# Two fully connected layers after a decaying attention: the second layer's products cut into halves of the array's rows

## The chip, the cores and the metric

One core of a Trainium2 chip (trn2) runs the whole program. The metric is device microseconds of one execution. Three runs of the kernel before took 862.36, 862.7 and 864.8 us (median 862.7). A TensorE product multiplies a stationary 128-row weight tile with moving columns; its sum goes to a bank of PSUM. The array can also be addressed as tiles of 64 of its 128 rows, which then hold weights of their own.

## The reference

Four sequences of 768 tokens and 8 heads of 48 pass a linear attention with decay; its 384 features per token pass two fully connected layers of width 2048, each `h = x @ w_in`, a pointwise function, `g @ w_out`:

```
h = x @ w_in;  g = max(h, 0) + alpha * min(h, 0);        x = g @ w_out     # first layer
h = x @ w_in;  g = h * tanh(log(1 + exp(h)));            out = g @ w_out   # second layer
```

## The kernel before

Each float32 operand is split into two float32r parts, high and low, and each product is made three times (`PASSES`: high by high, high by low, low by high). All sums are kept in float32.

The 3072 tokens are handled as 6 chunks of 512 columns, and the width as 16 blocks of 128: a layer has 96 slots, one for a chunk and a block. In a slot the **inner product** (tile `h`, one PSUM bank, two buffers) takes 3 row blocks x 3 passes = 9 products of 128 x 512 (`emit_h`, L269). The pointwise function makes g and its two parts `ghiB`, `gloB`. The **output sum** takes 3 banks (`acc0` to `acc2`, or `sc` and `yt` in turn) x 3 passes = 9 products of 128 x 512 (L690 in layer one, L817 in layer two). In the last chunk of layer two the operands change places, and a slot has 4 banks x 3 passes = 12 products of 128 x 384 (L815).

The work of the first layer and of the attention stands in an order by a table of places. Layer two, which the change touches, is written by the loop at the end: it goes in pairs of slots. For slots n and n + 1 it emits both inner products, then for each of the two the pointwise instructions (`mish`) and the output sum of four slots earlier (`LAG_B = 4`; in the first four slots these are the last four output sums of layer one). Each engine runs its instructions in the order in which they are emitted.

`mish(n)` has six ACT instructions (tanh of slot n, the first; a square of slot n; the high part of g of slot n - 2; two squares of slot n - 1 and one of slot n) and five of DVE (g of n - 2, b of n - 1, a of n, which is the last reader of bank `h`, the low part of g of n - 2, c of n - 1). The profile names these by the buffers that they share: tanh is `m`, its square `ghi`, the other squares `glo` and `s`. `split_x2` adds an ACT and a DVE instruction in three of 16 slots. `mB_turn` (DVE transposes, L825) empties a chunk's three banks after its last output sum; the last chunk's fourth bank is one of the two `sc` banks that the chunk before it has filled. `mB_last` orders the last two output sums bank by bank. GpSimd has two late weight splits (`w2_split`, emitted at slots 6 and 8) and no other work in layer two.

## Time and profile before

| | |
|---|---|
| median of 3 runs | 862.7 us |
| the profiled execution, its own time | 864.74 us |
| its span, first to last instruction | 862.8 us |
| TensorE busy | 854.3 us (99%) |
| DVE, ACT, GpSimd busy | 629.9, 612.3, 115.1 us |
| granted TensorE clock | 1.0 |

A timeline row holds the instructions of one kind that follow each other without a pause: start, length, count. A product's row is as long as it takes until its last column has left the array, so rows of products overlap, and the distance of their starts is what a product costs. An instruction's idle time before it, and what ended that, stand in brackets.

### The profile page before, as it was taken

What the parts mean: (1) busy time and instruction counts of PE and PEld (TensorE: products, weight loads), DVE (VectorE), ACT (ScalarE), POOL (GpSimd) and SP (SyncE); (2) the same over time, 40 slices, a digit from 0 to 9 for tenths busy, and PEclk for the clock granted to TensorE, in tenths of its full rate; (3) what the DMA queues carried; (4) which work ended last, traced back from release to release, by engine and by line L of the source; (5) the groups of instructions that cost most, each with busy time, mean ns of one, the idle gap of its engine ahead of it and who ended that gap; (6) DMA issues with size and microseconds to landing.
All of it is one profiled execution on the core that took longest, in us unless ns stands there. A gap on an engine that the chain in (4) does not pass through costs nothing.

```text
span 862.8 us, 16681 instructions
## 1 busy us (share of the span) xinstructions
PE 854.3 (99%) x6382; PEld 709.8 (82%) x6382; DVE 629.9 (73%) x969; ACT 612.3 (71%) x1170; POOL 115.1 (13%) x133
## 2 busy tenths in 40 slices
PE   9999999999999999999999999999999999999998
PEld 6887888888888888888888888888888888888897
DVE  8889776666656656444666887887887887887875
ACT  5987555445545445543556989989989998998886
POOL 5465641112211112100002000000000000000000
PEclk9999999999999999999999999999999999999999
DMA  9886734364255434223520300110110110100101
GB/s 347 260 247 179 223 99 133 96 206 135 84 163 162 147 85 171 66 65 120 172 78 15 111 1 1 32 43 1 30 45 1 29 47 0 30 9 1 28 10 38
DMA packets 65328, 79.95 MB, mean 93 GB/s; under 512 B 39648, under 2 KB 52448, under 8 KB 65248
## 3 DMA queue, kind: packets, MB, share of 16 engines
q1 hardware_dynamic: 64688, 78.78, 30.4%
q8 instruction: 50, 0.82, 0.4%
q14 instruction: 30, 0.25, 0.1%
q10 hardware_dynamic: 560, 0.10, 0.1%
HBM read 61.16 MB, written 15.73 MB: 89 GB/s over the span
## 4 chain that ended last, share of the span: by engine, by line
PE 92%; DVE 2%; ACT 2%; DMA 2%; issue 1%; POOL 0%; SPq 0%; DVEq 0%; ACTq 0%; POOLq 0%
PE h L269 43%; PE acc L690 21%; PE sc L817 8%; PE acc L817 8%; PE yt L817 4%; PE acc L815 2%; PE sc L501 1%; DMA nat<-in_nat 1%; PE h L532 1%; PE sc L815 1%; PE yt L553 1%; PE sc L546 1%; DMA cst<-in_consts 1%; PE yt L532 1%; ACT wrawr L216 0%
## 5 line engine op out<-in xcount | busy, mean ns | idle before, releaser
L269 PE MATMUL h<-x,w 128*128 128x512 f32 (+1 forms) x1746 | 415.5, 387 | 2.1 <-DVE x L190 1.9
L269 PEld LDWEIGHTS h<-x,w 128*128 128x128 f32 x1746 | 325.0, 188 | 69.7 <-issue 2.5
L690 PE MATMUL acc<-ghi,w 128*128 128x512 f32 x516 | 174.9, 394 | 0.0
L658 ACT ACTIVATE m<-h 128x512 f32<-128x512 f32 x96 | 57.1, 595 | 92.8 <-PE h L269 92.7
L660 DVE SCALAR_TENSOR_TENSOR g<-m,oma,h 128x512 f32<-128x512 f32 x96 | 71.6, 746 | 60.2 <-ACT m L658 59.2
L690 PEld LDWEIGHTS acc<-ghi,w 128*128 128x128 f32 x516 | 96.8, 188 | 21.3
L187 ACT ACTIVATE ghi<-g 128x512 fp32r<-128x512 f32 x86 | 54.2, 630 | 74.9 <-PE acc L690 48.0
L690 PE MATMUL acc<-glo,w 128*128 128x512 f32 x258 | 100.4, 389 | 0.0
L190 DVE TENSOR_TENSOR glo<-g,ghi 128x512 fp32r<-128x512 f32 x86 | 62.8, 730 | 51.5 <-ACT ghi L187 51.2
L754 DVE SCALAR_TENSOR_TENSOR a<-ghi,h 128x512 f32<-128x512 f32 x96 | 66.0, 687 | 38.5 <-ACT ghi L751 32.0
L754 DVE SCALAR_TENSOR_TENSOR g<-s,c 128x512 f32<-128x512 f32 x95 | 66.6, 701 | 22.5 <-ACT s L751 20.4
L762 ACT ACTIVATE m<-h 128x512 f32<-128x512 f32 x96 | 56.4, 588 | 35.6 <-PE h L269 35.6
L190 DVE TENSOR_TENSOR gloB<-g,ghiB 128x512 fp32r<-128x512 f32 x105 | 72.0, 685 | 7.1 <-ACT ghiB L187 7.1
L751 ACT ACTIVATE ghi<-m,biases 128x512 f32<-128x512 f32 x96 | 69.6, 725 | 3.2
L187 ACT ACTIVATE ghiB<-g 128x512 fp32r<-128x512 f32 x105 | 64.8, 617 | 9.1 <-PE acc L690 6.9
L751 ACT ACTIVATE glo<-ghi,biases 128x512 f32<-128x512 f32 x96 | 68.1, 709 | 0.1
L751 ACT ACTIVATE s<-glo,biases 128x512 f32<-128x512 f32 x96 | 68.1, 709 | 0.0
L751 ACT ACTIVATE s<-s,biases 128x512 f32<-128x512 f32 x96 | 68.0, 708 | 0.0
L817 PE MATMUL sc<-ghiB,w 128*128 128x512 f32 x192 | 66.9, 389 | 0.0
L754 DVE SCALAR_TENSOR_TENSOR b<-ghi,a 128x512 f32<-128x512 f32 x96 | 65.6, 684 | 0.1
L754 DVE SCALAR_TENSOR_TENSOR c<-glo,b 128x512 f32<-128x512 f32 x95 | 65.7, 691 | 0.0
L817 PE MATMUL acc<-ghiB,w 128*128 128x512 f32 x192 | 61.7, 389 | 0.0
(189 smaller groups left out, 1148.3 us busy)
## 6 DMA issues: line engine op xcount, KB each, us to landing
wrawr<-in_w SPq DMA_DIRECT2D x28, 768.0 KB, 5.3
nat<-in_nat SPq DMA_DIRECT2D x40, 288.0 KB, 4.4
w2d<-wj SPq DMA_DIRECT2D x16, 384.0 KB, 2.5
wraw<-w2d SPq DMA_DIRECT2D x16, 384.0 KB, 3.1
rk<-in_rkT SPq DMA_DIRECT2D x40, 128.0 KB, 3.1
x2d<-xo SPq DMA_DIRECT2D x6, 768.0 KB, 3.2
x<-x2d SPq DMA_DIRECT2D x6, 768.0 KB, 4.6
rk<-in_rkT SPq DMA_DIRECT2D x40, 96.0 KB, 2.8
```

What stands on the lines that cost most here:

```text
L187: act.activation(out=hi, in_=src, func=AF.Copy)
L190: eng.tensor_tensor(out=lo, in0=src, in1=hi.bitcast(F32), op=ALU.subtract)
L269: pe.matmul(h[:, n], w_in(layer, f, a, c), x[:, b, c, n], start=(k == 0), stop=(k == 3 * KC - 1))
L532: pe.matmul(y[i][64 * q:64 * q + 64, p * HC:(p + 1) * HC], T[ROWS[h], 2 * bp + i, k, :], pair[i][ROWS[h], 0, k, t], start=(r == 0 and not ...
L658: act.activation(out=m, in_=hA[s], func=AF.Relu, scale=-1.0)
L660: dve.scalar_tensor_tensor(out=g, in0=m, scalar=oma[:, f:f + 1], in1=hA.pop(s), op0=ALU.mult, op1=ALU.add)
L690: pe.matmul(acc[0][c], w_out(0, f, a)[:, c * 128:(c + 1) * 128], g[b], start=(f == 0 and k == 0), stop=(f == NF - 1 and k == 2))
L751: act.activation(out=out, in_=in_, func=AF.Square, scale=scale, bias=fin[bias])
L754: dve.scalar_tensor_tensor(out=out, in0=in0, scalar=scalar, in1=in1, op0=op0, op1=ALU.mult)
L762: act.activation(out=bnew("t", n), in_=v["h", n], func=AF.Tanh, scale=0.5)
L815: pe.matmul(acc[1][t][:, :DM], g[a][:, t * C:(t + 1) * C], w_out(1, f, b), **se)
L817: pe.matmul(acc[1][t], w_out(1, f, a)[:, t * 128:(t + 1) * 128], g[b], **se)
```

## The change

Layer two's main loop goes slot by slot, and each of its products is cut along the rows that it sums over: one product of rows 0 to 63 and one of rows 64 to 127, each with its own weight load. `rows_slot` writes two lanes, top and low. Top has the upper half of the slot's inner product, then the upper half of the output sum; low has first three lower halves left from the slot before, then the lower half of the output sum, then the lower half of the inner product but for its last three. The lanes are merged by a count of columns. So the two halves of one bank are never written at the same time: the first half's last product releases an event on GpSimd (`pool.nop()`, ordered behind it), and the second half's first product waits for that event. A slot has five such events, in the last chunk six (one for each bank of the output sum, one for the inner product, and one ahead of the next slot's output sum). `follow(m)`, with the pointwise work of slot m, comes once the three left products are issued. The last four output sums, two before `mB_last` and two in it, stay whole products.

TensorE, slot 4 of layer two. Before: the inner products of slots 4 and 5 (weights `w_5213`, `w_5236`), then the output sum of slot 0 (`w_5080`).

```order
L269 MATMUL h<-x,w_5213 128x512 [waits DVE_49]
L269 MATMUL h<-x,w_5213 128x512 x8
L269 MATMUL h<-x,w_5236 128x512 [waits DVE_49]
L269 MATMUL h<-x,w_5236 128x512 x8
L817 MATMUL sc<-ghiB,w_5080 128x512 [waits Activation_49]
L817 MATMUL sc<-gloB,w_5080 128x512
L817 MATMUL sc<-ghiB,w_5080 128x512 x2
L817 MATMUL sc<-gloB,w_5080 128x512
L817 MATMUL sc<-ghiB,w_5080 128x512
L817 MATMUL yt<-ghiB,w_5080 128x512
```

The same slot now. Halves of one product read alike; in a pair one is of the upper rows and one of the lower.

```order
L293 MATMUL sc<-ghiB,w_5080 128x512 [waits Pool_sequencer_49,Activation_49]
L293 MATMUL h<-x,w_5213 128x512
L293 MATMUL sc<-gloB,w_5080 128x512 [waits DVE_49]
...
L293 MATMUL sc<-gloB,w_5080 128x512
L293 MATMUL h<-x,w_5213 128x512
L293 MATMUL sc<-ghiB,w_5080 128x512
L293 MATMUL sc<-ghiB,w_5080 128x512 [waits Pool_sequencer_49]
L293 MATMUL yt<-ghiB,w_5080 128x512
L293 MATMUL sc<-gloB,w_5080 128x512
L293 MATMUL yt<-gloB,w_5080 128x512
L293 MATMUL sc<-ghiB,w_5080 128x512
L293 MATMUL yt<-ghiB,w_5080 128x512
L293 MATMUL sc<-ghiB,w_5080 128x512 [waits Pool_sequencer_49]
```

The output sum of slot 0 now lies beside the inner product of slot 4, and its second halves wait for GpSimd's event (`Pool_sequencer`).

DVE, where chunk 4's banks are emptied. Before:

```order
L754 SCALAR_TENSOR_TENSOR c<-glo,b 128x512
L825 STREAM_TRANSPOSE ot<-sc 128x512 [waits DMAHW4_49,DMAHW5_49,DMAHW3_49,DMAHW6_49,DMAHW2_49,DMAHW7_49,DMAHW0_49,PE_49]
L754 SCALAR_TENSOR_TENSOR g<-s_9139,c 128x512 [waits DVE_49,Activation_49]
L754 SCALAR_TENSOR_TENSOR b<-ghi,a 128x512
L754 SCALAR_TENSOR_TENSOR a<-ghi,h 128x512 [waits DVE_49,Activation_49]
L190 TENSOR_TENSOR gloB<-g,ghiB 128x512 [waits Activation_49]
L754 SCALAR_TENSOR_TENSOR c<-glo,b 128x512
L825 STREAM_TRANSPOSE ot<-sc 128x512
```

Now:

```order
L821 SCALAR_TENSOR_TENSOR c<-glo,b 128x512
L894 STREAM_TRANSPOSE ot<-sc 128x512 [waits PE_49]
L894 STREAM_TRANSPOSE ot<-sc 128x512
L821 SCALAR_TENSOR_TENSOR g<-s_11088,c 128x512 [waits DVE_49,Activation_49]
L821 SCALAR_TENSOR_TENSOR b<-ghi,a 128x512
L821 SCALAR_TENSOR_TENSOR a<-ghi,h 128x512 [waits DVE_49,Activation_49]
L190 TENSOR_TENSOR gloB<-g,ghiB 128x512 [waits Activation_49]
L821 SCALAR_TENSOR_TENSOR c<-glo,b 128x512
```

Both transposes of `sc` stand in one slot's work, where they stood in two.

TensorE, from the last inner product to `mB_last`. Before (`h` is slot 95's, then the output sums of slots 90, 91, 92, 93):

```order
L269 MATMUL h<-x,w_5163 128x512 x8
L815 MATMUL acc_9211<-w_5428,ghiB 128x384 [waits Activation_49]
...
L815 MATMUL acc_9211<-w_5730,ghiB 128x384 [waits Activation_49]
...
L815 MATMUL acc_9211<-w_5817,ghiB 128x384 [waits Activation_49]
...
L815 MATMUL acc_9211<-w_5043,ghiB 128x384 [waits Activation_49]
```

Now (the end of slot 95, its three left products, then the output sums of slots 92, 93 and, with `w_5062`, 94):

```order
L293 MATMUL h<-x,w_5163 128x512
L293 MATMUL sc<-w_5894,gloB 128x384
L293 MATMUL h<-x,w_5163 128x512 x3
L749 MATMUL acc_11059<-w_6027,ghiB 128x384 [waits Activation_49]
...
L749 MATMUL acc_11059<-w_5043,ghiB 128x384 [waits Activation_49]
...
L749 MATMUL acc_11059<-w_5062,ghiB 128x384 [waits Activation_49]
```

Two output sums stand behind the last inner product ahead of `mB_last`, where there were four.

```diff
--- before.py
+++ after.py
@@ -260,6 +260,67 @@
 
     PASSES = ((0, 0), (0, 1), (1, 0))
 
+    def h_products(layer, f, x, h):
+        steps = [(c, a, b) for c in range(KC) for a, b in PASSES]
+        return [(h, w_in(layer, f, a, c), x[:, b, c], k == 0, k == 3 * KC - 1) for k, (c, a, b) in enumerate(steps)]
+
+    def order(behind, ahead):
+        tc.add_manual_dep(behind.ins, ahead.ins.name,
+                          mybir.DependencyInfo(mybir.DependencyClass.Sync, mybir.DependencyReason.DATA), reason="turns")
+
+    late = 3
+    lower = {"h": [], "o": None}
+
+    def rows_slot(h, o):
+
+        nh, no = len(h), len(o)
+        per_bank = len(PASSES)
+        top = [("h", k, 0) for k in range(nh)] + [("o", k, 0) for k in range(no)]
+        low = [("o", k, 1) for k in range(no)] + [("h", k, 1) for k in range(nh)]
+        keep = low[len(low) - late:] if nh else []
+        low = [("tail", k, 1) for k in range(len(lower["h"]))] + low[:len(low) - len(keep)]
+        tail, lower["h"] = lower["h"], [h[k] for _, k, _ in keep]
+        marks = {}
+        mark_low = 6 if no > 3 * per_bank else 5
+        base = nh - len(keep)
+        clock = [0, 0]
+        lanes = [top, low]
+        while top or low:
+            lane = 0 if top and (not low or clock[0] <= clock[1]) else 1
+            kind, k, half = lanes[lane].pop(0)
+            out, w, x, start, stop = (tail if kind == "tail" else h if kind == "h" else o)[k]
+            first = lane if kind == "o" else 1 - lane
+            mm = pe.matmul(out, w[HALF[half]], x[HALF[half]], start=start and (lane == (kind == "o")),
+                           stop=stop and (lane != (kind == "o")))
+            clock[lane] += x.shape[-1]
+            mark = wait = None
+            if kind == "h" and lane == 0 and k == nh - 1:
+                mark = "h"
+            elif kind == "o" and lane == 1 and k % per_bank == per_bank - 1:
+                mark = "o", k // per_bank
+            elif lane == 1 and ((kind == "h" and k == mark_low) or (kind == "tail" and base_of[0] + k == mark_of[0])):
+                mark = "low"
+            if kind == "h" and lane == 1 and k == 0:
+                wait = marks["h"]
+            elif kind == "o" and lane == 0 and k % per_bank == 0:
+                wait = marks["o", k // per_bank]
+            elif kind == "o" and lane == 1 and k == 0:
+                wait = lower["o"]
+            if mark:
+                marks[mark] = pool.nop()
+                order(marks[mark], mm)
+                if mark == "low":
+                    lower["o"] = marks[mark]
+            if wait:
+                order(mm, wait)
+            if kind == "tail" and k == len(tail) - 1:
+                yield
+        base_of[0], mark_of[0] = base, mark_low
+        if not tail:
+            yield
+
+    base_of, mark_of = [0], [0]
+
     def emit_h(layer, f, x, h, n=slice(0, 512), which=None):
         steps = [(c, a, b) for c in range(KC) for a, b in PASSES]
         if which is not None:
@@ -681,14 +742,19 @@
         gA[s] = (hi, lo)
 
     def mA_out(s):
+        whole(out_products(s))
+
+    def whole(products):
+        for o, w, x, start, stop in products:
+            pe.matmul(o, w, x, start=start, stop=stop)
+
+    def out_products(s):
         blk, f = A_SLOTS[s]
         if f == 0:
             acc[0] = [bank(f"acc{c}") for c in range(KC)]
         g = gA.pop(s)
-        for c in range(KC):
-            for k, (a, b) in enumerate(PASSES):
-                pe.matmul(acc[0][c], w_out(0, f, a)[:, c * 128:(c + 1) * 128], g[b],
-                          start=(f == 0 and k == 0), stop=(f == NF - 1 and k == 2))
+        return [(acc[0][c], w_out(0, f, a)[:, c * 128:(c + 1) * 128], g[b], f == 0 and k == 0, f == NF - 1 and k == 2)
+                for c in range(KC) for k, (a, b) in enumerate(PASSES)]
 
     def mA_end(blk):
         o = per.tile([128, KC, 512], F32, tag="wraw", name="xo", bufs=NRAW)
@@ -736,7 +802,8 @@
 
     def mB_h(s):
         j, f = B_SLOTS[s]
-        v["h", s] = emit_h(1, f, fin["x", j], bank("h", 2))
+        v["h", s] = bank("h", 2)
+        return h_products(1, f, fin["x", j], v["h", s])
 
     OLD = {"t": "m", "gb": "g", "q": "ghi", "s1": "glo"}
 
@@ -808,13 +875,15 @@
         if f == 0:
             acc[1] = acc_B[j] = banks_B(j)
         g = v["g", s]
+        products = []
         for t in parts if j == NCH - 1 else range(KC):
             for k, (a, b) in enumerate(PASSES):
-                se = dict(start=(f == 0 and k == 0), stop=(f == NF - 1 and k == 2))
+                se = f == 0 and k == 0, f == NF - 1 and k == 2
                 if j == NCH - 1:
-                    pe.matmul(acc[1][t][:, :DM], g[a][:, t * C:(t + 1) * C], w_out(1, f, b), **se)
+                    products.append((acc[1][t][:, :DM], g[a][:, t * C:(t + 1) * C], w_out(1, f, b)) + se)
                 else:
-                    pe.matmul(acc[1][t], w_out(1, f, a)[:, t * 128:(t + 1) * 128], g[b], **se)
+                    products.append((acc[1][t], w_out(1, f, a)[:, t * 128:(t + 1) * 128], g[b]) + se)
+        return products
 
     def mB_turn(j, c):
 
@@ -848,7 +917,7 @@
     def mB_last():
 
         for s, t in ((2, 0), (2, 1), (1, 0), (2, 2), (1, 1), (2, 3), (1, 2), (1, 3)):
-            mB_out(NB - s, (t,))
+            whole(mB_out(NB - s, (t,)))
             if s == 1:
                 mB_end(NCH - 1, (t,))
 
@@ -1022,37 +1091,39 @@
         run_plan()
 
 
-        for n in range(0, NB + LAG_B, 2):
-            pair = range(n, n + 2)
-            for m in pair:
-                if m < NB:
-                    mB_h(m)
-            if n == 0:
-                mA_hi(NA - 1)
-                mA_lo(NA - 1)
-            for m in pair:
-                if m < LAG_B:
-                    mA_out(NA - LAG_B + m)
-                mish(m)
-                if m == LAG_B - 1:
-                    mA_end(NCH - 1)
-                if m in (6, 8):
-                    w2_split(11 + (m - 6) // 2, pool)
-                if m == 4:
-                    load_x2(1)
-                if m == NB + LAG_B - 1:
-                    mB_last()
-                elif LAG_B <= m < NB + LAG_B - 2:
-                    mB_out(m - LAG_B)
-                    j, f = divmod(m - LAG_B + 1, NF)
-                    if j and f < KC:
-                        mB_turn(j - 1, f)
-                if m < NB:
-                    j, f = B_SLOTS[m]
-                    if f in (5, 7, 9) and j + 1 < NCH:
-                        split_x2(j + 1, (f - 5) // 2)
-                    if f == 10 and j + 2 < NCH:
-                        load_x2(j + 2)
+        def follow(m):
+
+            mish(m)
+            if m == LAG_B - 1:
+                mA_end(NCH - 1)
+            if m in (6, 8):
+                w2_split(11 + (m - 6) // 2, pool)
+            if m == 4:
+                load_x2(1)
+            j, f = divmod(m - LAG_B + 1, NF)
+            if j and f < KC and m < NB + LAG_B - 2:
+                for c in (range(2), (), (2,))[f] if j == NCH - 1 else (f,):
+                    mB_turn(j - 1, c)
+            if m < NB:
+                j, f = B_SLOTS[m]
+                if f in (5, 7, 9) and j + 1 < NCH:
+                    split_x2(j + 1, (f - 5) // 2)
+                if f == 10 and j + 2 < NCH:
+                    load_x2(j + 2)
+
+        mA_hi(NA - 1)
+        mA_lo(NA - 1)
+        for m in range(NB):
+            for _ in rows_slot(mB_h(m), mB_out(m - LAG_B) if m >= LAG_B else out_products(NA - LAG_B + m)):
+                if m:
+                    follow(m - 1)
+        for _ in rows_slot([], []):
+            follow(NB - 1)
+        for m in range(NB, NB + LAG_B):
+            if m < NB + LAG_B - 2:
+                whole(mB_out(m - LAG_B))
+            follow(m)
+        mB_last()
 
 
 # ---- launch: one core ----
```

## Rows read from the trace of the kernel before

**Rows 1.** The page's first lines: the span, and each engine's busy time.

```profile
span 862.8 us, 16681 instructions
...
PE 854.3 (99%) x6382; PEld 709.8 (82%) x6382; DVE 629.9 (73%) x969; ACT 612.3 (71%) x1170; POOL 115.1 (13%) x133
```

**Rows 2.** Chain that ended last: start us, us, engine, tile, line, count.

```profile
600.14 4.08 PE acc L817 x18
```

**Rows 3.** By shape, PE: line, operation, shape, count | busy us, mean ns | idle.

```profile
L269 PE MATMUL h<-x,w 128*128 128x512 f32 x1710 | 410.6, 390 | 2.1 <-DVE x L190 1.9 <-DVE w L190 0.2
...
L269 PE MATMUL h<-x,w 128*128 128x256 f32 x36 | 4.8, 288 | 0.0
...
L377 PE MATMUL acc<-RK,cst 64*48 64x256 f32 x2 | 0.6, 376 | 0.0
```

**Rows 4.** Timeline, PE, the opening: start us, us, engine, line, operation, shape, count.

```profile
27.73 2.68 PE L269 MATMUL h<-x,w 128*128 128x256 f32 x21
```

**Rows 5.** By shape, PE, 5.8 to 7 us, the warm-up products in float32.

```profile
L641 PE MATMUL acc<-ghi 128*128 128x384 f32 x5 | 1.8, 486 | 0.0
```

**Rows 6.** Timeline, PE, the same warm-up products.

```profile
5.29 2.10 PE L641 MATMUL acc<-ghi 128*128 128x384 f32 x6
```

**Rows 7.** Timeline, PE: float32 products in tiles of 64 rows, 64 columns.

```profile
10.38 0.61 PE L377 MATMUL acc<-RK,cst 64*48 64x256 f32 x8
...
117.75 0.65 PE L501 MATMUL sc<-rk 48*64 48x64 f32 x32
118.22 0.49 PE L546 MATMUL sc<-nat 64*48 64x48 f32 x27
```

**Rows 8.** Timeline, 380.17 to 380.75 us: TensorE, GpSimd, TensorE.

```profile
380.17 0.22 PE L532 MATMUL yt<-rk,T 48*64 48x64 f32 x1
380.54 0.11 POOL L536 MEMSET T<- 112x8 f32 x1 [17.47 <-PE yt L532]
380.70 0.13 PEld L532 LDWEIGHTS yt<-rk,T 48*64 48x64 f32 x1 [0.46 <-POOL T L536]
```

**Rows 9.** Timeline, ACT, the end of one slot and the start of the next.

```profile
603.00 0.62 ACT L187 ACTIVATE ghiB<-g 128x512 fp32r<-128x512 f32 x1
...
606.30 0.60 ACT L762 ACTIVATE m<-h 128x512 f32<-128x512 f32 x1 [0.84 <-PE h L269]
...
607.56 0.61 ACT L187 ACTIVATE ghiB<-g 128x512 fp32r<-128x512 f32 x1
```

**Rows 10.** Timeline, DVE, beside them.

```profile
607.69 0.69 DVE L754 SCALAR_TENSOR_TENSOR a<-ghi,h 128x512 f32<-128x512 f32 x1 [0.71 <-ACT ghi L751]
608.29 0.69 DVE L190 TENSOR_TENSOR gloB<-g,ghiB 128x512 fp32r<-128x512 f32 x1
```

**Rows 11.** Timeline, PE, the change from whole products to tiles.

```profile
115.79 1.75 PE L269 MATMUL h<-x,w 128*128 128x512 f32 x7
117.47 0.27 PE L532 MATMUL h<-rk,T 48*64 48x64 f32 x1
```

**Rows 12.** Timeline, GpSimd, the two last weight splits.

```profile
457.41 0.82 POOL L236 CAST w<-wraw 128x768 fp32r<-128x768 f32 x1 [68.61 <-PE acc L690]
458.32 2.17 POOL L190 TENSOR_TENSOR w<-wraw,w 128x768 fp32r<-128x768 f32 x1
```

**Rows 13.** Timeline, DVE, the last chunk's first slots.

```profile
805.34 0.71 DVE L825 STREAM_TRANSPOSE ot<-sc 128x512 f32<-128x512 f32 x1
```

**Rows 14.** Timeline, PE, the same place.

```profile
806.10 0.62 PE L815 MATMUL sc<-w,ghiB 128*128 128x384 f32 x2 [0.37 <-DVE ot L825]
```

**Rows 15.** Timeline, ACT, the end.

```profile
847.94 0.57 ACT L762 ACTIVATE m<-h 128x512 f32<-128x512 f32 x1
...
853.86 0.63 ACT L187 ACTIVATE ghiB<-g 128x512 fp32r<-128x512 f32 x1 [0.70 <-DVE g L754]
```

**Rows 16.** Timeline, DVE, the end.

```profile
854.52 0.69 DVE L190 TENSOR_TENSOR gloB<-g,ghiB 128x512 fp32r<-128x512 f32 x1 [0.44 <-ACT ghiB L187]
```

**Rows 17.** Timeline, PE, the end.

```profile
855.27 0.44 PE L815 MATMUL acc<-w,gloB 128*128 128x384 f32 x1
```

## The prediction

> **What bounds the kernel now.** I read the page's first lines, then the chain of waits, then products by shape, then timelines of single places. TensorE is busy 854.3 of 862.8 us [rows 1], at a granted clock of 1.0 throughout, the 2.4 GHz level, so the time is the number of products by the distance of their starts. In layer two 18 products of 512 columns take 4.08 us [rows 2], 226.7 ns each. A column per cycle makes 213.3 ns; 13.4 are left. They don't depend on the width: 21 products of 256 columns lie in 2.68 us, the last alone being 288 ns long [rows 3, 4], so 119.6 ns from start to start, of which 106.7 are columns and 12.9 are not. Float32 products of the whole array, with a weight load each, hardly have this part: six of 384 columns in 2.10 us, the last 486 ns [rows 5, 6], are 323 ns apart, 320 of them two cycles a column. So some 13 ns per product belong to float32r on the whole array, and the reader should see that only they can be won: nothing in TensorE's row is a wait.
>
> The next engine is ACT. From the high part at 603.00 to its idle time (0.84 us before 606.30) are 2.46 us, and from tanh at 606.30 to the next high part 1.26 [rows 9]: 3.7 us a slot against 4.08. It has room down to that.
>
> **What the change does, part by part.** *Products.* Halves are made of 96 x 9 inner products, 4 x 9 output sums of layer one, 80 x 9 of 512 columns and 12 x 12 of 384 in layer two: 1764. Two halves side by side need as many cycles as one whole product, if the tiles run at once. No float32r tile of 64 rows is in the trace, so I bound its step from both sides. That tiles run at once is shown in float32: 32 products of 64 columns in four tiles take 118.22 - 117.75 = 0.47 us, 59 ns for four, where columns alone would be 4 x 53 in sequence [rows 7]. What they lose at a change of weights is small: eight of 256 columns lie in 0.61 us, the last 376 ns long [rows 3, 7], so the second round of four starts about 0.22 us after the first, 213.3 for columns and 3 to 7 ns more; by the 59 ns it is 5. One end is therefore 216 ns for a pair (3 lost), the other 227 to 229 (the 13 ns stay in each tile, some ns for twice the instructions). The nearest row by form, two row tiles in turn, is the 3 to 7 ns: I take 218, a saving of 8.7 ns by 1764 products = **15.3 us** (216: 18.9; 220: 11.8; 228: -2.3). A slot is then 18 x 0.218 = 3.92 us, still above ACT's 3.7.
>
> The Trainium skill (TensorE: Matmul & The Clock Gate, Back-to-back issue gap) gives 2.5 ns beyond the columns as the gap between products, so 215.8 for 512. The 226.7 above do not follow it, the float32 rows do; by that rule in both tiles the saving would be 19.2 us, about my fast end.
>
> *Events.* Each event lies four pairs ahead of its waiter, 0.87 us. The way through GpSimd is in the attention: a product that starts at 380.17 and ends at 380.39, the memset at 380.54 for 0.11, the next load at 380.70 [rows 8]: 0.15 to GpSimd and 0.05 back, with 0 to 0.11 for the event itself. With the product's own 0.39 [rows 3] that is 0.59 to 0.70 us. Its weight load takes under 0.12 (256-column products come every 119.6 ns with one load each), so it may start 0.75 after the event's product. I take no wait. If the load has to stand a full pair ahead (0.65), up to 0.05 us is lost at the four places of a slot where TensorE waits for events: 0.05 x 4 x 96 = 19 us is the other end. Behind a waiting product the whole TensorE queue stands, both lanes.
>
> *GpSimd's splits* at slots 6 and 8 now lie between events: 0.82 and 2.17 us [rows 12]. The first event behind them is wanted for the ninth pair, 1.96 us into the slot. If events pass a running instruction, only the 0.82 hold them: nothing; if not, some 1.4 us each. I take 0 (to 2.8).
>
> *Later g and h.* tanh now starts 0.87 us into the next slot (three left halves, the last one's 0.39 and its hand-over). From there a, the last reader of bank h, is done 2.08 later and the low part of g 2.68 [rows 9, 10]: 2.95 and 3.55 us into the slot, wanted at 3.92 and 4.8. About 1 us of cover remains where before there were several; a split of x (one ACT instruction more) takes 0.6 of it and gives it back. I count nothing.
>
> *Banks of chunk 4.* DVE's first transpose follows c, which follows the low part of g by a step of 0.60: tanh + 3.2 us, so 4.06 us into slot 84, done at 4.77 [rows 10, 13]. The low lane wants the `sc` bank after three halves of 512 and nine of 384 columns, 3 x 0.218 + 9 x 0.165 = 2.14. TensorE waits 2.7 us (3.3 if for both transposes); now it is 0.37 [rows 14]. **+2.6.**
>
> *The end.* Before, lo of slot 94 let TensorE go on at 855.27, 7.33 us after tanh of slot 95 at 847.94 [rows 15 to 17], and TensorE had four output sums to fill it, which left about 0.4 us idle. Now two sums do. From the start of slot 95, tanh comes at 4.80 (3.94 of slot, two of the left halves at 0.218, 0.39 and hand-over), so lo of 94 lets TensorE go on at 12.13. TensorE's sums 92 and 93, 24 whole products of 384 columns at 173 ns, run from 4.7 to 8.9, with 0.4 for g of 93; then it waits from 9.6 on. Without waits the third product of sum 94 would start at 9.2. **+2.9 - 0.4 = 2.5.**
>
> *Fill and switches.* Three halves run alone at the last slot, three places are empty in the first: 3 x 0.218 = **0.65**. Whole products to tiles cost 0.1: seven products in 1.75 us put the last start at 117.15, the first tile starts 0.32 later instead of 0.227 [rows 3, 11]; twice, **0.2**.
>
> Sum: -15.3 + 2.6 + 2.5 + 0.65 + 0.2 = -9.3. Against the profiled execution's own 864.7 us this is 855.4; that execution lies 2.0 above the median 862.7, so against the median **853.4**.
>
> **Rivals.** *The 13 ns stay in each tile.* For it: they did not depend on the width, so they could be a fixed time in which new weights come in, which a tile of its own would have as well; float32 tiles save nothing over float32 on the whole array. Against: nothing but the float32 rows. The pair then takes 226.7 to 229, and the 6 us of costs stand alone: 862.7 + 6 to 10 = **869 to 873**, slower. It decides from a pair of 224 ns on, where saving (4.8 us) and costs (6) cross.
> *Half of them goes*, a pair of 221 to 225: saving 3 to 10, time **859 to 866**.
> *Weight loads of the two lanes queue.* 256-column products bound a load by 119.6 ns, two in turn by 239: 12.5 x 1764 = 22 us more and 6 of costs, **890**. Against it stands the 59 ns for four products with four loads [rows 7]. The Trainium skill (same page, LDWEIGHTS) says that a load's time goes by its columns, not its rows, 107 ns for 128; so the halves double the loads' time, and two in turn, 213, would just hide. No run here has shown 128-column loads in two tiles.
> *Events come late*, by up to 0.05 us each: 19 us on the forecast, **872**. Against it: the 0.75 us that the load may have.
> *The tiles don't run at once* in float32r: 1764 products more, **1260**; rows 7 speak against it, but at half the column rate.
>
> **How the numbers follow.** Forecast 0.56: from 862.7 - 18.9 + 4.5 = 848 to 862.7 - 11.8 + 8.8 = 860. Half goes 0.12, the 13 ns stay 0.21, loads queue 0.04, late events 0.05, no overlap 0.02. Range 847 to 872: it leaves out queueing loads, no overlap and a part of the slow rival. Within 0.3% (2.6 us, about what three runs tell apart) is 860.1 to 865.3: half of "half goes", 0.06. Faster: the forecast and most of the rest of "half goes", 0.61. Slower: 0.33.
>
> **What would show it.** In the timeline of layer two, pairs of products start 216 to 220 ns apart, the second some ns behind the first, and 18 pairs take 3.9 us; pairs 227 apart mean the slow rival, 239 queueing loads. TensorE's waits should name DVE once at slot 84 (near 2.7 us) and ACT and DVE at the end (near 3), and GpSimd not at all; idle time before GpSimd's name, or around slots 7 and 9, makes the events' cost wrong. ACT should be idle 0.2 us a slot before tanh; if not, ACT has become the bound. If the clock falls below 1.0, all of this is wrong.

## The result, and the profile after

The changed kernel takes 875.14 us (median of 4 runs, 872.82 to 876.0) against 862.94 of the kernel before on the same chip: ratio 1.0133, 95% interval 1.0108 to 1.0159. It is 1.3% slower; forecast was 853.4, with a range of 847 to 872. The profiled execution took 876.0 us, 11.3 more than that of before (864.7).

The page of the changed kernel: its first lines and the granted clock in 40 slices (answers to [rows 1]).

```profile
span 874.3 us, 20799 instructions
...
PE 860.6 (98%) x8146; PEld 753.9 (86%) x8146; DVE 629.3 (72%) x969; ACT 617.4 (71%) x1170; POOL 116.3 (13%) x133
...
PEclk9999999999999999999999999999999999999998
```

The 1764 products more are there. TensorE's idle time has grown, but by far too little to hide a gain of 15 us. So the first thing to look at is the step. Busy time and instruction counts of a stretch without waits, of the changed kernel and then of the kernel before:

```profile
520.00:600.00 80.00, 80.00 (x709) 77.90 (x707) 66.02 (x105) 73.61 (x121) 0.00 (x0) 1.00 0.10 21
```

```profile
520.00:600.00 80.00, 80.00 (x355) 66.26 (x354) 65.70 (x104) 72.50 (x122) 0.00 (x0) 1.00 0.10 21
```

In the same 80 us stand 709 halves or 355 whole products (the fourth number's count, PE): 354.5 pairs against 355, 226 ns each either way. Finer, by the start of tanh 64 slots apart (ACT, timeline of the changed kernel, then of before):

```profile
529.70 0.60 ACT L829 ACTIVATE m<-h 128x512 f32<-128x512 f32 x1 [0.36 <-PE h L293]
...
790.91 0.60 ACT L829 ACTIVATE m<-h 128x512 f32<-128x512 f32 x1 [0.36 <-PE h L293]
```

```profile
524.70 0.60 ACT L762 ACTIVATE m<-h 128x512 f32<-128x512 f32 x1 [0.84 <-PE h L269]
...
785.82 0.60 ACT L762 ACTIVATE m<-h 128x512 f32<-128x512 f32 x1 [0.84 <-PE h L269]
```

261.21 / 64 = 4.081 us a slot with halves, 261.12 / 64 = 4.080 without. Both lanes run at once and hide their loads and events; a pair costs what one product of the whole array did, to the nanosecond. Nothing is saved.

What TensorE waited for in layer two (PE's and its weight loads' waits; us in total, times, longest):

```profile
PE sc L293 <- DVE ot L894: 2.9, 1, 2.9
PE h L293 <- DVE a L821: 2.8, 2, 1.5
PE acc L749 <- ACT ghiB L187: 1.4, 1, 1.4
```

```profile
PEld acc L293 <- POOLq L310: 0.4, 2, 0.2
```

The events on GpSimd (L310) hold it these 0.4 us, and 0.3 in a row for `h`. The wait at `sc` is the forecast one of slot 84 ([rows 14] before: 0.37). The two waits for `a` were not forecast. They stand ahead of the first products of slots 8 and 10, and the timeline of GpSimd, DVE and TensorE in the changed kernel shows why:

```profile
485.87 1.85 POOL L190 TENSOR_TENSOR w<-wraw,w 128x768 fp32r<-128x768 f32 x1
...
495.88 2.17 POOL L190 TENSOR_TENSOR w<-wraw,w 128x768 fp32r<-128x768 f32 x1
```

```profile
486.34 1.93 DVE L190 TENSOR_TENSOR x<-x,x 128x512 fp32r<-128x512 f32 x1 [1.53 <-ACT x L187]
...
496.27 2.33 DVE L821 SCALAR_TENSOR_TENSOR g<-s,c 128x512 f32<-128x512 f32 x1
```

```profile
490.32 0.74 PE L293 MATMUL h<-x,w 64*128 64x512 f32 x4 [1.52 <-DVE a L821]
```

A DVE step of 0.7 us that meets GpSimd's subtraction ends 0.55 us after it: 1.93 and 2.33 us. The delay reaches a, the last reader of bank `h`, and TensorE. Before, GpSimd ran these splits at 457 and 463 us, as soon as TensorE had released them ([rows 12]), with nothing of x near; now they stand in its queue behind the events of the slots before them. The Trainium skill (SBUF — State Buffer, SBUF: two separate sides) describes this: DVE with two SBUF inputs and GpSimd share a pair of ports, which one of them holds for its whole instruction. The trace agrees, with 1.93 us for a step of 0.74.

Ahead of slot 8 the late splits did a second thing. Until GpSimd has split them, the raw weights keep two of the three `wraw` buffers, so the load of the next chunk's x waits for the third, which the store of layer one's last result holds. SyncE's wait in the changed kernel, and what ACT then waits for:

```profile
SPq L781 <- DMA x2d<-xo: 2.9, 1, 2.9
```

```profile
485.68 0.63 ACT L187 ACTIVATE x<-x 128x512 fp32r<-128x512 f32 x1 [0.59 <-DMA x<-x2d]
```

So DVE's low part of x not only takes 1.2 us more at 486.34, it also starts some 0.7 us later than in the run a_splits below, where the load does not wait.

The last new thing is the clock. Behind the wait at slot 84 the granted clock falls to the 1.2 GHz level for 3.4 us; products of 512 columns then start 0.425 us apart (two steps in the rows below), and near the end ten products of 384 columns 0.32 us apart. Windows of the changed kernel (the column before the last two is the clock), and TensorE's timeline in two of them:

```profile
800.00:812.00 12.00, 9.09 (x72) 8.46 (x70) 7.51 (x13) 6.46 (x11) 0.00 (x0) 0.86 0.08 12
860.00:870.00 10.00, 8.40 (x37) 7.45 (x36) 6.01 (x10) 5.18 (x9) 0.00 (x0) 0.83 0.05 20
```

```profile
808.48 0.62 PE L293 MATMUL h<-x,w 64*128 64x512 f32 x1
...
809.33 0.62 PE L293 MATMUL h<-x,w 64*128 64x512 f32 x1
...
866.38 0.52 PE L749 MATMUL acc<-w,gloB 128*128 128x384 f32 x1
866.70 0.84 PE L749 MATMUL acc<-w,ghiB 128*128 128x384 f32 x2
```

This holds a hint. 512 columns at 1.2 GHz are 426.7 ns and 384 are 320.0: at the lower level the fixed 13 ns are gone. Whatever they are, they don't belong to a product as such.

### The profile page after: what moved, and what is told of

Same layout as the page of the kernel before. It is cut to its first block, busy times and chain, and to the rows that moved or that the text cites. A ratio compares the mean times of both kernels' runs of the same rounds, so it can differ in the third digit from the quotient of the medians.

```text
span 874.3 us, 20799 instructions
## 1 busy us (share of the span) xinstructions
PE 860.6 (98%) x8146; PEld 753.9 (86%) x8146; DVE 629.3 (72%) x969; ACT 617.4 (71%) x1170; POOL 116.3 (13%) x133
## 4 chain that ended last, share of the span: by engine, by line
PE 92%; ACT 3%; DVE 2%; DMA 2%; issue 1%; SPq 0%; POOL 0%; DVEq 0%; ACTq 0%; POOLq 0%
PE acc L749 22%; PE h L293 22%; PE h L330 21%; PE acc L293 10%; PE sc L293 7%; PE yt L293 3%; PE sc L562 1%; PE h L593 1%; PE yt L614 1%; PE sc L607 1%; DMA cst<-in_consts 1%; PE yt L593 1%; DMA x<-x2d 1%; ACT s L818 0%; DVE g L821 0%
## 5 line engine op out<-in xcount | busy, mean ns | idle before, releaser
L293 PE MATMUL h<-x,w 64*128 64x512 f32 x1728 | 342.9, 389 | 2.8 <-DVE a L821 2.8
L293 PEld LDWEIGHTS h<-x,w 64*128 64x128 f32 x1728 | 274.3, 185 | 15.9 <-DVE a L821 3.6
L330 PE MATMUL h<-x,w 128*128 128x512 f32 (+1 forms) x882 | 211.5, 386 | 0.2 <-DVE w L190 0.2
L330 PEld LDWEIGHTS h<-x,w 128*128 128x128 f32 x882 | 163.0, 188 | 34.0 <-DVE w L190 0.6
L293 PE MATMUL sc<-ghiB,w 64*128 64x512 f32 x384 | 124.1, 386 | 0.0
L293 PE MATMUL acc<-ghiB,w 64*128 64x512 f32 x432 | 117.9, 387 | 0.0
L293 PE MATMUL sc<-gloB,w 64*128 64x512 f32 x192 | 74.2, 386 | 0.0
L293 PE MATMUL yt<-ghiB,w 64*128 64x512 f32 x192 | 74.2, 386 | 0.0
L293 PEld LDWEIGHTS sc<-ghiB,w 64*128 64x128 f32 x384 | 70.7, 184 | 3.1
L293 PEld LDWEIGHTS acc<-ghiB,w 64*128 64x128 f32 x432 | 69.5, 184 | 3.0 <-POOLq L310 0.4
```

Of the source, the lines that this page charges most:

```text
L293: mm = pe.matmul(out, w[HALF[half]], x[HALF[half]], start=start and (lane == (kind == "o")), stop=stop and (lane != (kind == "o")))
L330: pe.matmul(h[:, n], w_in(layer, f, a, c), x[:, b, c, n], start=(k == 0), stop=(k == 3 * KC - 1))
```

## The experiments

Two questions: what are the 13 ns, and are three places the whole loss?

**m1: products alone.** A small program with 36 products of each form, one form after the other.

```
for k in range(36): pe.matmul(b1, w[:, 0], x[:, 0], ...)                      # L53: same weights, same columns
for k in range(36): pe.matmul((b0, b1)[k % 2], w[:, k % 12], x[:, k % 6], start=True, stop=True)      # L56
for k in range(36):
    for i in range(2): pe.matmul((b0, b1)[i], w[HALF[i], k % 12], x[HALF[i], k % 6], ...)   # L66; L69 one half, L73 quarters
wb, xb: the same in bfloat16                                                  # L76 whole, L83 halves
```

> Products alone, 36 of each form, other weights and other columns each time unless said; the rest of the computation is left out. What carries the 13 ns that a float32r product of the whole array takes beyond its columns? Theory A (the fixed part belongs to each product of a tile at the 2.4 GHz level, whatever the rows, the weights and the bank): float32r of 512 columns 226.7 ns from start to start with other weights, with the same weights, with sums begun and ended each time, with 64 columns of weights, in one tile of 64 rows, and in each of two or four tiles in turn; 128 columns 66.7. Rival B (it is the exchange of the weights): 213 to 216 with the same weights each time, more than 226.7 where loads of several tiles meet. Rival C (it is the accumulation in one bank): 213 to 216 where each product begins its own sum in the other bank. Rival D (it is the delivery of 4-byte columns at a column per cycle; after's 64-row halves took 426.6 and 320.0 ns, no more than their columns, while the clock was at the 1.2 GHz level): bfloat16 of 512 columns at 213 to 216 and of 256 at 107 to 109, float32r everywhere 226.7. Under A bfloat16 takes 226.7 and 120.

TensorE's timeline (start, length of the row, shape of the tile, count):

```profile
39.39 8.32 PE L53 MATMUL b<-x,w 128*128 128x512 f32 x36
47.55 8.32 PE L56 MATMUL b<-x,w 128*128 128x512 f32 x36
68.05 8.45 PE L66 MATMUL b<-x,w 64*128 64x512 f32 x72
76.34 8.32 PE L69 MATMUL b<-x,w 64*128 64x512 f32 x36
84.59 8.48 PE L73 MATMUL b<-x,w 32*128 32x512 f32 x144
93.22 7.72 PE L76 MATMUL b<-xb,wb 128*128 128x512 bf16 x35 [0.16 <-issue]
104.80 7.94 PE L83 MATMUL b<-xb,wb 64*128 64x512 bf16 x72
```

Two shorter windows of L83, from its second pair on:

```profile
105.03 0.59 PE L83 MATMUL b<-xb,wb 64*128 64x512 bf16 x4
105.03 7.07 PE L83 MATMUL b<-xb,wb 64*128 64x512 bf16 x63
```

A row is its steps and one last product (0.39 us, bfloat16 0.38). Float32r takes (8.32 - 0.39) / 35 = 226.6 ns with other weights, with the same weights, with a bank each time, and in one half of the rows. For halves the steps are those of pairs: four halves in 0.59 us leave one step of 0.21 us beside the last one's 0.38, where even starts would need three of 0.11; so the two of a pair start together. A pair in float32r takes (8.45 - 0.39 - 0.11) / 35 = 227 ns, where 0.11 is what the first step, at the switch from whole products to tiles, is longer; four quarters take 227 to 228. So neither accumulation nor rows carry the 13 ns, and rival C falls. The same weights were still loaded each time (36 loads of 188 ns), so this row does not settle rival B; m2 does, with 216 ns and other weights each time. Two forms of theory A missed by more: 128 columns come every 112 ns, not 66.7, and with 64 columns of weights 512 columns take 230.

Bfloat16 takes 7.34 / 34 = 215.9 (35 of 36 products are in the record), and a pair of halves (7.07 - 0.38) / 31 = 215.8. Rival D holds in its main part: the extra goes with 4-byte columns. But halves save nothing in bfloat16 either: of the 2.5 ns that a product takes there beyond its columns, a pair of halves gives none back.

**m2: how the columns are read.** The same program; L60 reads one float32r column 512 times, L63 every second of 1024.

```
x[:, k % 6, 0:1].to_broadcast([128, 512])       # L60
pairs[:, k % 3, :, k % 2]                       # L63; pairs is x seen as [.., 512, 2]
```

> Products alone again, 36 of each form; the rest of the computation is left out. The products alone of the run before showed 226.7 ns for every float32r form of 512 columns and 215.8 for bfloat16 (213.1 a pair in two tiles of 64 rows). Is the part beyond the columns fixed for 4-byte columns, or is it the reading of them from SBUF? Theory (fixed per product of 4-byte columns at the 2.4 GHz level, whatever stands where): float32r of 512, 384 and 256 columns 226.7, 173.3, 119.9 to 120; one column read 512 times and every second column also 226.7. Rival (SBUF gives 4-byte columns too slowly, or a first read waits): one column read 512 times 213 to 217, every second column more than 226.7, 240 and up. In bfloat16 two tiles of 64 rows should take off the 2.5 ns of the whole array at any width: 384 columns 162.5 whole and 160 a pair; 128 columns 56 whole, and a pair 53 to 56, or more if the two loads of 95 ns don't overlap any more.

```profile
44.65 4.47 PE L57 MATMUL b<-x,w 128*128 128x256 f32 x36
48.95 7.94 PE L60 MATMUL b<-x,w 128*128 128x512 f32 x36
56.73 16.50 PE L63 MATMUL b<-x,w 128*128 128x512 f32 x36
73.05 6.04 PE L66 MATMUL b<-xb,wb 128*128 128x384 bf16 x36
79.03 6.02 PE L70 MATMUL b<-xb,wb 64*128 64x384 bf16 x72
```

The theory as written (fixed per product of 4-byte columns) falls, the rival holds: one column read 512 times takes (7.94 - 0.38) / 35 = 216.0, every second column (16.50 - 0.63) / 35 = 453, twice 226.7. 256 columns take (4.47 - 0.28) / 35 = 119.7, 13 over their 106.7, so the extra is one per product. The 13 ns hang on how the moving columns lie in SBUF; that TensorE waits for SBUF in them is my reading, no row names it. In bfloat16, 384 columns (L66 whole, L70 halves) take 163 ns whole and 163 a pair, and 128 columns 56 either way: the 2.5 ns that halves should have taken off stay. The 213.1 that the expectation gives for m1's pair came from dividing the row by 35.5 steps, as if halves started evenly; a pair starts together.

**m3: bytes or elements?** Bfloat16 with every second column spans the same 2048 bytes per partition as 512 float32r columns (L63 whole, L67 halves); 256 float32r columns read twice each span half of that (L54); one float32r column in halves (L59).

> Products alone a third time, 36 of each form; the rest of the computation is left out. The second showed 215.9 ns for float32r where one column is read 512 times, 226.7 for 512 columns side by side and 453 for every second column. Theory (what a product has to fetch from SBUF sets the extra: the row of bytes that the columns span): bfloat16 with every second column spans the 2048 bytes of 512 float32r columns and takes 226.7, whole and in two tiles of 64 rows; float32r with 256 columns read twice each spans half and takes 215.8; one float32r column read 512 times in two tiles of 64 rows takes 213.1 to 213.4 a pair, as bfloat16 did, so that halves save 2.5 ns wherever the fetch is not the limit. Rival (it is the 4-byte element itself, and one column only escapes by being one address): bfloat16 with every second column 215.8 whole and 213 a pair; 256 columns read twice 226.7.

```profile
38.72 7.93 PE L54 MATMUL b<-x,w 128*128 128x512 f32 x36
46.58 8.04 PE L59 MATMUL b<-x,w 64*128 64x512 f32 x72
54.79 8.06 PE L63 MATMUL b<-xb,wb 128*128 128x512 bf16 x35 [0.17 <-issue]
62.78 8.30 PE L67 MATMUL b<-xb,wb 64*128 64x512 bf16 x72
```

The span decides: bfloat16 with a gap takes (8.06 - 0.39) / 34 = 225.6, against 215.9 side by side; float32r with half the bytes takes 215.7. A pair of halves again takes what a whole product does: (8.30 - 0.39) / 35 = 226 with the gap, and for one float32r column (8.04 - 0.38 - 0.10) / 35 = 216, with 0.10 for the switch to tiles. So the expectation's 213 for that pair did not come: halves save nothing where the fetch is not the limit either. The rule of the step is then: 2.5 ns beyond the columns, and about 13 where the columns lie 4 bytes apart at the 2.4 GHz level, for whole products and for pairs of halves alike. The Trainium skill (TensorE: Matmul & The Clock Gate, Back-to-back issue gap) gives the 2.5 alone; that agrees with bfloat16 here and not with float32r side by side.

**a_splits: GpSimd's two splits early.** The changed kernel with one place moved:

```
-            if m in (6, 8):
-                w2_split(11 + (m - 6) // 2, pool)
+            if m in (0, 2):
+                w2_split(11 + m // 2, pool)
```

> The changed kernel with GpSimd's two splits of second-layer weights moved from slots 6 and 8 to slots 0 and 2 (GpSimd's queue), where no split of x is near. Theory (while GpSimd's subtraction runs, DVE's low part of x stands still: 1.93 us instead of 0.74 at 486.34; that moves a late and TensorE waits 1.7 and 1.4 us for bank h at 488.4 and 498.4, with 0.1 each for the restart): both waits go, 875.1 - 3.3 = 871.8, and TensorE waits for DVE only at slot 84. Rival (GpSimd's events stand behind its running subtraction): the waits move to slots 1 and 3 with GpSimd's name, 1.4 us each, and the time stays near 875. The theory allows a small part of the second, since DVE's steps meet the subtraction in slots 1 and 3 as well: up to 873.

871.88 us (870.98 to 872.6), ratio to before 1.0105 [1.0090, 1.0121]. TensorE's waits in layer two:

```profile
PE sc L293 <- DVE ot L894: 2.9, 1, 2.9
PE acc L749 <- ACT ghiB L187: 1.4, 1, 1.4
```

The waits for `a` are gone and 3.3 us with them, as the theory had it; none with GpSimd's name has come. The edit takes away both the collision and the late load of x (issued at 478.26 us instead of 481.14), so it does not tell them apart. Ahead of slot 8, `a` starts at 487.58 us instead of 489.58; of these 2.0 us the trace gives 1.2 to the collision and the rest to the load.

**a_turn: chunk 4's transposes ahead.** In `follow`, `mB_turn` for banks 0 and 1 comes before `mish(83)` instead of behind it.

> The changed kernel with DVE's two transposes of chunk 4 ahead of slot 83's activation steps instead of behind them. Theory (TensorE stands 3.07 us at 804.5 only because the transposes stand behind c in DVE's queue, and the clock's fall to the 1.2 GHz level for 3.4 us behind it, 1.7 us of work, comes from that wait): 875.1 - 4.8 = 870.3, granted clock 1.0 there. DVE's and ACT's later steps of that slot are 1.3 us later, of which about 1 us is covered, so 0 to 0.5 comes back as a wait for bank h. Rival (the fall of the clock has nothing to do with the wait): 872.0. Rival (the wait moves on to bank h and g at slots 85 and 86 in full): 874 to 875.

869.43 us (869.35 to 869.66), ratio 1.0078 [1.0061, 1.0095]; 5.7 less than the changed kernel, 0.9 more than expected. `sc` is no longer waited for, and the longest waits left are the two for `a`, 2.8 us.

The clock stayed at 0.999 to 1.0 in all four runs, at the end too, where the changed kernel's profiled run lost 1.5 us by it; that accounts for the 0.9 and more.

**a_end: the last two slots as before.**

```
-        for m in range(NB):                 # halves
+        for m in range(NB - 2):
...
+        for m in (NB - 2, NB - 1):
+            whole(mB_h(m))
```

> The changed kernel with the last two slots in whole products and in the order of before (inner products of 94 and 95 together, then the sums of 90 and 91). Theory (the end's waits come from sum 94 and 95 having only two sums of other slots to cover them): the wait of 1.54 us at 862.7 goes and with it the 1.2 GHz level at 866.4 to 869.6 (10 products at 320 instead of 173 ns, 1.5 us), about 0.5 of restarts too: 875.1 - 3.5 = 871.6. Rival (the end is late by itself, since tanh of slot 95 comes late whatever stands before): the wait stays at 1 us or more, 874 to 875.

874.77 us (871.82 to 875.06), ratio 1.0132 [1.0114, 1.0150]: no gain that can be told. The wait stayed, 1.00 us. ACT's timeline, tanh of slots 93 and 95 (that of 94 stands half way):

```profile
848.00 0.60 ACT L829 ACTIVATE m<-h 128x512 f32<-128x512 f32 x1 [0.47 <-PE h L293]
...
855.22 0.57 ACT L829 ACTIVATE m<-h 128x512 f32<-128x512 f32 x1
```

The rival was right. With three lower halves of 93 left over, its tanh starts only when the last pair of slots begins, and ACT, at 3.6 us a slot, then has three slots to do where it had two: that is read from this timeline. It fits that a_all, whose pairs begin four slots earlier, has no such wait. In a_end's profiled run TensorE stood at slot 84 as long as in the changed kernel, and the clock did not fall, so the fall follows such a wait in some runs and not in others (of the changed kernel's four runs, 872.82 us had a clock of 1.0 and the other three 0.995 to 0.998):

```profile
800.00:812.00 12.00, 9.10 (x90) 8.41 (x87) 7.84 (x13) 7.81 (x14) 0.00 (x0) 1.00 0.09 14
```

**a_all and a_whole: all three places, with and without halves.** a_all has the two edits above and the last six slots in whole pairs. a_whole differs in slots 0 to 89 alone:

```
         for m in range(NB - 6):
-            for _ in rows_slot(mB_h(m), mB_out(m - LAG_B) if m >= LAG_B else out_products(NA - LAG_B + m)):
-                if m:
-                    follow(m - 1)
-        for _ in rows_slot([], []):
-            follow(NB - 7)
+            whole(mB_h(m))
+            whole(mB_out(m - LAG_B) if m >= LAG_B else out_products(NA - LAG_B + m))
+            follow(m)
```

> The changed kernel with GpSimd's two splits at slots 0 and 2, DVE's two transposes ahead of slot 83's steps, and the last six slots in whole products in pairs as before the change; slots 0 to 89 in halves. Theory (a pair of halves takes 226.7 ns as one whole product did, and what the change cost are waits at three places): 875.1 - 3.3 (splits, measured) - 5.7 (transposes with the clock, measured) - 2.1 (the end: 2.6 us of gaps against 0.5 before) = 864.0; left above before are three halves of fill twice alone, 0.65, two switches, 0.2, and some 0.3 of waits for events. Rival (halves cost by themselves in every slot, by events and by the lanes' offset): 866 or more, with gaps all along layer two. Rival (halves give something that the waits had hidden): 861 or less.

> As the run before (splits, transposes, last six slots), but slots 0 to 89 in whole products too, slot by slot: inner products of a slot, then the output sums of the slot four behind; no halves, no events. Theory (the step is the same with or without halves): 862.6 to 863.1, before's time, and 0.9 to 1.3 less than with halves. Rival (the order slot by slot, not the halves, costs: only half a slot stands between inner products and the next use of their bank): waits for bank h along layer two, 864 or more. Rival (halves save something): this one is slower than the one with halves.

a_all: 864.25 us (10 runs, 863.63 to 868.51), ratio 1.0023 [1.0009, 1.0038], 864.0 expected. a_whole: 862.4 us (10 runs), ratio 0.9992 [0.9978, 1.0006]. No PE row waits in layer two in either. The same window in both, a_all first:

```profile
520.00:600.00 80.00, 80.00 (x710) 79.99 (x708) 65.95 (x105) 73.69 (x121) 0.00 (x0) 1.00 0.10 21
```

```profile
520.00:600.00 80.00, 80.00 (x355) 66.24 (x354) 66.01 (x105) 73.91 (x122) 0.00 (x0) 1.00 0.10 21
```

With the three places mended, 10.9 of the 12.2 us are back, and 710 halves are 355 products again. What the halves still cost is the difference of the two, 1.85 us by the medians. The spans of the profiled runs (862.3, 861.9) are only 0.4 apart, but a_whole's run stood in layer one, where the two do not differ, and a_all's did not:

```profile
PE h L330 <- DVE x L190: 1.5, 1, 1.5
```

From the first product of layer two (455.43 and 456.64 us) to the end are 406.9 and 405.2 us, so 1.7 us, more than the 0.9 to 1.3 expected. a_whole is as fast as before, not faster: no version here beats it.

**b_held: the collision without halves.** The kernel before, with an event ahead of each of GpSimd's splits that waits for the last inner product of slots 7 and 9.

```
+                    tc.add_manual_dep(pool.nop().ins, last[0].ins.name, ...)   # last inner product emitted
                     w2_split(11 + (m - 6) // 2, pool)
```

> The kernel before with GpSimd held back: each of its two splits of second-layer weights waits for the last inner product of slot 7 or 9 (an event on GpSimd ahead of it), about where the changed kernel runs them, instead of at 457 and 463 us. Theory (before's order by pairs has the cover that the changed order lacks): DVE's steps beside the subtraction take 1.3 to 2.2 us instead of 0.7, and TensorE does not wait: 862.6. Rival (the collision costs wherever it stands among the splits of x): TensorE waits 1 to 1.7 us after each, 864.6 to 866.

864.44 us (10 runs, 863.42 to 866.0), ratio 1.0014 [1.0001, 1.0026].

```profile
493.87 2.17 POOL L190 TENSOR_TENSOR w<-wraw,w 128x768 fp32r<-128x768 f32 x1
```

```profile
494.44 0.69 DVE L756 SCALAR_TENSOR_TENSOR a<-ghi,h 128x512 f32<-128x512 f32 x1
495.04 1.55 DVE L190 TENSOR_TENSOR gloB<-g,ghiB 128x512 fp32r<-128x512 f32 x1
```

```profile
499.53 0.70 PE L271 MATMUL h<-x,w 128*128 128x512 f32 x2 [0.86 <-DVE a L756]
```

Between the two. Beside the first split a DVE step of 0.7 us takes 2.33, and TensorE does not wait; behind the second it waits once, 0.86 us. Of DVE's steps beside the second, `a`, which reads `h` from PSUM, keeps its 0.69 us, and the low part of g, with both inputs in SBUF, takes 1.55. So late splits cost in the old order too: about 1 us by the trace, 1.6 by the medians (interval 0.1 to 2.2), of the 3.3. That the rest came from the changed order's smaller cover fits this, but no run isolates it.

## Why the prediction was wrong

**The step that failed** is the choice of the product's step: "The nearest row by form, two row tiles in turn, is the 3 to 7 ns: I take 218", a saving of 15.3 us. It was 226.7 and 0. The row chosen was a tile like the new ones, but of float32, whose columns run at half the rate; rows 5 and 6, which gave a whole float32 product only 3 ns, share that. Float32 tiles with 3 to 7 ns beside whole float32 products with 3 said that tiles take nothing off, as the first rival noted, and that slow columns have no 13 ns. m1 to m3 show that the 13 ns come with 4 bytes from column to column in SBUF, and that a pair of halves takes the step of one whole product in each of the five forms compared: 227 in float32r, 216 and 163 in bfloat16, 226 in bfloat16 with a gap, 216 for one float32r column. The first rival, "The 13 ns stay in each tile", had it right with 0.21, for a reason that was wrong (a fixed time for new weights; with new weights each time one float32r column takes 216). Its 869 to 873 is below the 875.1 measured, by two costs that no case had.

The sum, by the profiled executions:

| term | forecast | measured |
|---|---|---|
| 1764 products | -15.3 | 0.1 (4.081 for 4.080 us a slot), and 0.5 for 12 slots of the last chunk (tanh of slot 86 to that of slot 94: 33.54 us for 33.23) |
| GpSimd's splits | 0 (to 2.8) | 3.3 (2 waits and what follows them; a_splits gives 3.3) |
| slot 84's wait | +2.6 | 3.2 - 0.6 of before = 2.6 |
| 1.2 GHz behind it | none | 1.7 (half of 3.4 us) |
| end | +2.5 | about 2.2, and 1.5 for ten products at 320 instead of 173 ns |
| fill, switches, events | 0.85 | 0.85 taken over, 0.3 for events |

That is 13.0. The two executions differ by 11.3 us, but that of before stood 1.9 us in layer one ([rows 3], `x` of DVE; "nothing in TensorE's row is a wait" passes over it), and the changed one did not. Their first products of layer two, before and now:

```profile
457.18 4.24 PE L269 MATMUL h<-x,w 128*128 128x512 f32 x18
```

```profile
455.53 0.49 PE L293 MATMUL h<-x,w 64*128 64x512 f32 x1
```

From there to the end of the span are 405.7 and 418.8 us: 13.1, as the terms have it. Why halves of 512 and 384 columns side by side cost 0.04 us a slot in the last chunk was not looked into.

**Slot 84**: the mechanism and its size were right, and a_turn removed it by the named cause, DVE's order. **The splits**: the forecast priced events standing behind GpSimd's instruction; in fact the instruction moved behind the events, into DVE's way, and kept the buffers that the load of x could have taken. What would have told the first of these stood in DVE's timeline of before, beside GpSimd's cast at 463.53 (0.82 us) and subtraction at 464.44 (2.16), which I had not read:

```profile
463.59 1.31 DVE L754 SCALAR_TENSOR_TENSOR c<-glo,b 128x512 f32<-128x512 f32 x1
465.01 2.15 DVE L754 SCALAR_TENSOR_TENSOR g<-s,c 128x512 f32<-128x512 f32 x1
```

**Events**: right, 0.7 us in all (0.4 and 0.3) instead of up to 19. **Loads queue** and **tiles don't run at once**: right to reject; the two loads of a pair, some 185 ns each in the profile's rows, start 4 ns apart in m1 and overlap. **End**: right in mechanism, and a_end adds that ACT's backlog of one slot sets it. **Later g and h**: "about 1 us of cover" was right in size, and too little for the 2.0 us by which `a` came late ahead of slot 8. **The clock**: "if it falls below 1.0, all of this is wrong" named it and gave it no price; the two falls cost 1.7 and 1.5 us.

## What to carry to other kernels

Before pricing a fixed part of an instruction by a neighbouring row, ask what makes it, and compare each form with its own counterpart: tiles of float32 with whole products of float32, not with whole products of float32r. Cutting the rows of an array that is already full saved nothing in float32r and nothing in bfloat16 here: the two halves start together, and together they take the time of one whole product. And when an engine is given signals to pass on, look at what it did before in its free time: that work now waits for the signals, and lands somewhere else.

## What was not expected of the hardware

- A product's extra time over its columns follows the bytes from one moving column to the next: 226.7 ns for 512 columns 4 bytes apart in float32r, 225.6 in bfloat16 with a gap after each column, 216 for 2 bytes a column (bfloat16 side by side, float32r with each column read twice) and for one column read over and over, 453 for 8 bytes. At the 1.2 GHz level it is gone (steps of 0.425 us for 512 columns, 0.32 for 384).
- Two tiles of 64 rows take the step of one whole product in bfloat16 as well, 215.8 ns a pair against 215.9.
- A DVE step with two SBUF inputs stands still while GpSimd subtracts: 1.93 to 2.33 us for 0.7; with one input in PSUM it does not, 0.69.
- After a wait of 2.9 us the granted clock fell to 1.2 GHz in one profiled run and stayed at 2.4 in another of the same stretch.
